# The outputs of a chunked delta rule made in transposed form by the matmuls themselves

## The chip, the cores and the metric

The kernel runs on one core of one Trainium2 chip. The metric is device microseconds for one execution, and the smaller it is the better. The engines that matter here are TensorE (PE, matmuls; its weight loads are listed as PEld), VectorE (DVE), ScalarE (ACT), GpSimd (POOL) and SyncE (SP), which issues DMAs. Each engine runs its own list of instructions in order; semaphores tie the lists together. Matmuls write PSUM, a small memory of banks that PE adds into; everything else lives in SBUF, which has 128 partitions.

## The reference, cut to what matters

There are 4 batches, 8 heads, 768 tokens and 48 numbers to a head. Each (batch, head) carries a 48 x 48 state through its tokens; the outputs of the heads, side by side (8 x 48 = 384), are the rows of a feed-forward layer.

```python
for t in range(S):
    y[:, :, t] = einsum('bhd,bhde->bhe', q[:, :, t], state)
    v_old = einsum('bhde,bhd->bhe', state, k_n[:, :, t])     # k_n: k of length 1
    state = state + beta_t * einsum('bhd,bhe->bhde', k_n[:, :, t], v_t - v_old)
x = y.transpose(0, 2, 1, 3).reshape(3072, 384)
out = gelu_exact(x @ w_in) @ w_out      # w_in 384 x 2048, w_out 2048 x 384, float64 in memory
```

## The kernel before

**Tiling.** The tokens are cut into 12 chunks (c = 0 to 11) of C = 64. A chunk has two units (a = 0, 1); a unit is two batches, whose 2 x 64 tokens fill the 128 partitions. Inside a chunk the recurrence is solved in closed form, as small matmuls, one for each batch and head. Heads go in four pairs j, r being the head within the pair and p the batch within the unit; D = 48, H = 8, NP = 4 pairs, NM = 3 blocks of 128 model columns, NF = 16 blocks of 128 hidden columns.

**The state steps of a chunk**, in order (`state_steps`, L792):

- `against_state` (L651): the product psK (L667) of both units: Kt (keys, transposed: the head's numbers in partitions, tokens in columns) and Qt (queries, likewise) are weights of 48 rows and 64 columns, the state St of 48 columns moves through them. Each unit has its own PSUM tile, for the key half and the query half.
- `subtract` (L672): DVE makes W from psK and V; ACT copies the query half out of PSUM as `y` (L679), 128 x 384 in one copy a unit. L684 is the second step of W on DVE.
- `solve` (L691): psU = Zf . W (L702), and ACT's copies of it, `U` (L710, L712). Zf is the inverse of a triangular matrix of the chunk, made ahead for two chunks at a time.
- `outputs` (L760): `use` (L717) makes psY = P . U (L732), with P (tokens by tokens, masked) as weights of 64 columns and U of 48 columns moving; `update` makes the step of the state (L743); `next_state` adds it to St on DVE; `read` (L750) makes x = psY + y on DVE, three additions a unit (L758). For chunks 0 and 1 `read` is three copies on ACT.
- `turns` (L782): six transposes of 128 x 128 on PE (L788), x being tokens by model columns, into the PSUM tile psX, and one ACT copy, 128 x 768, to xT (model columns by tokens), for which the layer waits. Chunks 0, 1 and 2 use `turn` (L766) instead, one call a unit; in chunk 1, y is added there by PE.

**Made ahead.** `load_blocks` brings keys and queries as 32 x 32 blocks; `turned_k` (L397, L399) and `turned_q` (L402) transpose them on DVE to Kt and Qt. Kt has six slots, that is three chunks. `grams` (L419) makes psG = Kt . Kt, `queries` (L437) psP = Kt . Qt, which DVE multiplies by the mask to P (L450). The helper `products` (L414) does the matmuls of both, 64 columns and 64 moving, so the profile shows both under the name psG. psG's copies to SBUF are queued with `put_off` and given out by `copy_out` (L570) at times of the plan. The rows of the triangular inverse are pairs of DVE instructions (L501, L503), its joining is psJ (L593), with 32-row operands.

**The layer.** For chunks 2 to 11 the two matrix products of the layer (fc1: xT by w_in, fc2: the result by w_out) are made in a form with seven products in place of eight, on halves. `mix_x` (L879) makes the sums of xT on DVE (L884); the parts are called P1, P5, P6, P2, R11, P7, R22, P3, R12, P4 and R21 (`part_of_layer`, L906), in four blocks of four hidden columns (psX, psZ, psY, psV, L916), then the second layer (L859). P7 writes psY, DVE adds pu into G from it (L947), and P4 writes the same PSUM again. `behind` chains all these products to one line on PE, so none can overtake another. Chunks 0 and 1 have the plain form (fc1 L811 psH, fc2 L829 psO).

**Order.** The layer of chunk w - 1 is made while the state steps of chunk w run; such a stage is some 46 to 51 us. A written plan (L1196 to L1304) gives each step a due time in units of stages (`at`, L1054; `state_at`, L1189, for the state steps), and `emit` (L1062) writes the instructions in the order of these times. DVE runs in exactly that order (`manual_schedule`, last lines). `together` (L623) chains the PE instructions of several steps, `keep` (L899) holds an ACT instruction at its place; the order of PE, ACT and SP is otherwise the scheduler's. The plan's lines that matter: even stages have `join_steps` j0, j1, j2 for the pair of chunks (w, w + 1) and the grams of w + 2 and w + 3; odd stages have none. `query(w)` is the queries' product of chunk w.

**PSUM.** The pool `dn` (L72) has two slots of two banks each; psK, psU, psY with psS, psG, psP, psJ and psX of `turns` take turns in them. `mlp`, `z` and `sq` belong to the layer.

**w_in.** It comes as 64-bit numbers by 24 DMAs on SP (`fetch`, L202 and L213), three for each of 8 parts of 256 hidden columns, one for each block of 128 model rows, and is decoded on DVE, ACT and POOL in the first stages.

Of the kernel before, what the change touches and what calls it, by code (L numbers as in the profile page):

```python
# [8 lines left out]
F32 = mybir.dt.float32  # L9
U32 = mybir.dt.uint32  # L10
# [9 lines left out]
def kernel(  # L20
# [35 lines left out]
    NA = B // 2  # L56
    NG = NC // 2
    NU = 2 * NA * H
    NM = DM // 128
    NF = DF // 128  # L60
    HALF = [slice(0, C), slice(C, 2 * C)]
# [10 lines left out]
    def dn(name):  # L72
        return ps.tile([128, 2, 512], F32, tag="dn", name=name)
# [109 lines left out]
    St = cpool.tile([128, NA, 2, NP, D], F32)  # L183
    nc.vector.memset(St, 0.0)
    nc.scalar.activation(lim[:, 1:2], lim[:, 0:1], ACT.Gelu)

    beta_m = cpool.tile([128, NC, NA, H], F32)


    win = moe_w_in.bitcast(U32).rearrange("(m q) (g f w) -> q g m f w", q=128, f=WC, w=2)  # L190
    wout = moe_w_out.bitcast(U32).rearrange("(f q) (n w) -> q f n w", q=128, w=2)
    w_parts = [(w_in_sb[:, g], win[:, g]) for g in range(DF // WC)]
# [9 lines left out]
    def fetch(n):  # L202
        if n >= len(w_parts):
            return
        dst, src = w_parts[n]
        if n < n_in:
            raw = stage[:, n % NS * 2 * WG:(n % NS + 1) * 2 * WG]
        else:
            raw = slots[(n - n_in) % len(slots)]
        w_raw[n] = raw.rearrange("q (n w) -> q n w", w=2)  # L210
        raw = raw.rearrange("q (m n w) -> q m n w", m=dst.shape[1], w=2)
        for m in range(dst.shape[1]):
            nc.sync.dma_start(out=raw[:, m], in_=src[:, m])  # L213
# [81 lines left out]
    def heads(ap):  # L295
        return ap.rearrange("q (j r) d -> q r j d", r=2)
# [348 lines left out]
    def pairs(ap, s):  # L645

        return ap.rearrange("q (k s r) d -> q k s r d", s=2, r=2)[:, :, s]
# [3 lines left out]
    def against_state(us):  # L651

        for u in us:
            u.W = wk.tile([128, H, D], F32, tag="W", name="W")
            u.y = None
            if u.c == 0:
                nc.gpsimd.tensor_tensor(u.W, u.V,
                                        ng[:, u.a].unsqueeze(2).to_broadcast([128, H, D]),
                                        op=ALU.mult)
                continue  # L660
            u.psK = dn("psK")[:, :, 0:2 * NP * D].rearrange("q r (x j d) -> q x r j d", x=2, d=D)
            for x in range(2):
                for j in range(NP):
                    for r, p in QUADS:
                        rows = slice(r * C, r * C + D)
                        to = HALF[p ^ (j % 2)] if x and u.c > 1 else HALF[p]
                        nc.tensor.matmul(u.psK[to, x, r, j, :], lhsT=(u.Qt if x else u.Kt)[rows, p, j, :],  # L667
                                         rhs=St[rows, u.a, p ^ r, j, :], start=True, stop=True)
        if us[0].c > 2:
            subtract(us)  # L670

    def subtract(us):  # L672

        for u in us:
            if u.c == 0:
                continue
            u.y = wk.tile([128, H, D], F32, tag="y", name="y")
            nc.vector.tensor_tensor(heads(u.W), u.psK[:, 0], heads(u.V), op=ALU.subtract)
            nc.scalar.copy(heads(u.y), u.psK[:, 1])  # L679
        for u in us:  # L680
            if u.c == 0:
                continue
            gm = gms[u.c // 2][:, u.t]
            nc.vector.tensor_tensor(u.W, u.W, gm.unsqueeze(2).to_broadcast([128, H, D]),  # L684
                                    op=ALU.mult)
# [4 lines left out]

    def solve(us, copies=(nc.scalar.copy, nc.scalar.copy)):  # L691
        psU = dn("psU")
        for u in us:
            zf = Zf[(u.c // 2) % 2]
            if u.c == 0 and u.a:
                psU = dn("psU")
            u.psU = quarters(psU[:, :, u.a * NP * D:(u.a + 1) * NP * D])
            for k in range(NP // 2):
                for r in range(2):
                    for p, s in SIDES:  # L700
                        h = 4 * k + 2 * s + r
                        nc.tensor.matmul(u.psU[HALF[p ^ s], s, k, r, :],  # L702
                                         lhsT=zf[HALF[p], u.t * H + h, :],
                                         rhs=u.W[HALF[p], h, :], start=True, stop=True)
        for u, copy in zip(us, copies):
            solved(u, copy)
# [41 lines left out]
            nc.vector.tensor_tensor(St[:, u.a], St[:, u.a], u.psS, op=ALU.add)  # L748

    def read(u, copy=nc.scalar.copy):  # L750
        u.x = wk.tile([128, H, D], F32, tag="x", name="x")
        both = slice(0, 128)
        for to, at_, s in ((both, both, 0), (HALF[0], HALF[1], 1), (HALF[1], HALF[0], 1)):
            dst, src = pairs(u.x[to], s), u.psY[s][at_]
            if u.c < 2:
                copy(dst, src)
            else:
                nc.vector.tensor_tensor(dst, src, pairs(u.y[at_], s), op=ALU.add)  # L758

    def outputs(us):  # L760
        use(us)
# [4 lines left out]
    def turn(u):  # L766
        if u.a == 0:
            xTs[u.c] = wk.tile([128, NM, NA * 128], F32, tag="xT", name="xT")
        xT = xTs[u.c]
        psX = sq("psX", NM, 128)  # L770
        for m in range(NM):
            cols = slice(m * 128, (m + 1) * 128)
            if u.c == 1:

                for i, part in enumerate((u.x, u.y)):
                    nc.tensor.matmul(psX[:, m, :], lhsT=part.rearrange("q h d -> q (h d)")[:, cols],
                                     rhs=ident, start=i == 0, stop=i == 1)
            else:
                nc.tensor.transpose(psX[:, m, :], u.x.rearrange("q h d -> q (h d)")[:, cols], ident)
        nc.scalar.copy(xT[:, :, u.a * 128:(u.a + 1) * 128], psX)  # L780

    def turns(us):  # L782
        c = us[0].c
        xT = xTs[c] = wk.tile([128, NM, NA * 128], F32, tag="xT", name="xT")
        psX = dn("psX")[:, :, 0:DM].rearrange("q a (m n) -> q a m n", n=128)
        for u in us:
            for m in range(NM):
                nc.tensor.transpose(psX[:, u.a, m, :],  # L788
                                    u.x.rearrange("q h d -> q (h d)")[:, m * 128:(m + 1) * 128], ident)
        keep(nc.scalar.copy, xT.rearrange("q m (a n) -> q a m n", n=128), psX)  # L790

    def state_steps(c, first=(), second=()):  # L792
        us = [tiles[c, a] for a in range(NA)]
        return [(together, (against_state, us), *first), (together, (solve, us), *second),
                (outputs, us), (together, (turns, us))]


    FH = NF // 2
# [390 lines left out]
    def state_at(c, *times, first=(), second=()):  # L1189

        steps = state_steps(c, first, second)
        if len(times) > len(steps):
            steps = steps[:-1] + [(turn, tiles[c, a]) for a in range(NA)]
        return [(t, step) for t, step in zip(times, steps) if t is not None]

    plan = [at(c + 1 + 0.25 * (c == 1), c + 2 + 0.25 * (c == 0), ffn_steps(c)) for c in range(NC)]  # L1196
# [30 lines left out]
    for c in range(4, NC):  # L1227
# [37 lines left out]
    for w in range(3, NC):  # L1265
        two_ahead = w + 2 < NC
        if w % 2:
# [10 lines left out]
            elif two_ahead:  # L1278
# [56 lines left out]
```

## Time and profile before

| what | value |
|---|---|
| median of 3 runs | 639.91 us (639.57 to 640.15) |
| the profiled execution: first to last instruction (span) | 638.7 us |
| mean granted clock of PE, as a share of full speed | 0.985 |
| instructions in the trace | 22156 |
| busy share of PE, DVE, ACT, POOL | 97%, 78%, 41%, 10% |
| L902 on ACT, copy of psX to xT, 9 of them | 0.80 us each; ACT idle 124.3 us before them in sum |
| data moved by DMA | 39.79 MB, 62 GB/s on the mean |

The profiled execution has no time of its own beside its span, which lies 1.2 us under the median. Times of single instructions below count from the span's start. In the lines of a profile, `out<-in` are the names of the tiles, `128*128` the weights' rows by columns, `128x192` the moving tile, and `x16` the number of instructions in the group; each float32 matmul of the code is two instructions. A matmul's busy time overlaps that of the next, so what one costs is read from start to start. On the page the tenths are the busy share of 40 slices, 16 us each. `[0.28 <-PE psK L667]` behind a line is the time that the engine had waited, and for what.

### The profile page before, as it was taken

To read this page: it belongs to the slowest core of one execution; us is meant where nothing else is said; L and a number is where in the kernel's file an instruction comes from. 1 tells how busy PE (TensorE), PEld (TensorE's weight loads), DVE (VectorE), ACT (ScalarE), POOL (GpSimd) and SP (SyncE) were. 2 spreads that over 40 slices of the span, in tenths; PEclk is the share of its full clock that TensorE was granted. 3 is DMA by queue.
4 is the path that set the end of the run, shared out by engine and by line. 5 is a ranking of instruction groups with operands and counts; after the bars stand their busy time and mean duration, and the time that the engine had idled before them with its cause. 6 is when DMAs were issued, how large, how long until landed. Compare 5 with 4: busy or idle time off the path is not lost.

```text
span 638.7 us, 22156 instructions
## 1 busy us (share of the span) xinstructions
PE 618.4 (97%) x9702; PEld 573.8 (90%) x9702; DVE 496.6 (78%) x1011; ACT 259.9 (41%) x586; POOL 64.9 (10%) x58
## 2 busy tenths in 40 slices
PE   6779999999999999999999999999999999999997
PEld 5667776776899999999999999999999999999997
DVE  6999989999799987999677999577999565354342
ACT  3576877624541265132265132265142253231230
POOL 4044002100300012001012001012001000000000
PEclk9977999999999999999999999999999999999999
DMA  9794884303442234221335222311222300100101
GB/s 134 172 280 139 149 175 137 50 1 73 73 67 44 47 51 77 56 36 36 58 48 79 54 27 47 57 27 28 52 29 38 62 4 2 26 2 3 26 2 25
DMA packets 158433, 39.79 MB, mean 62 GB/s; under 512 B 150016, under 2 KB 153216, under 8 KB 158336
## 3 DMA queue, kind: packets, MB, share of 16 engines
q1 hardware_dynamic: 155664, 37.34, 30.2%
q8 instruction: 76, 1.25, 0.8%
q10 hardware_dynamic: 2672, 1.03, 0.8%
q14 instruction: 21, 0.17, 0.1%
HBM read 33.62 MB, written 4.72 MB: 60 GB/s over the span
## 4 chain that ended last, share of the span: by engine, by line
PE 81%; DVE 11%; ACT 2%; DMA 2%; issue 2%; POOL 0%; SPq 0%; DVEq 0%; ACTq 0%; POOLq 0%
PE psX L859 12%; PE psY L916 11%; PE psX L916 8%; PE psY L859 8%; PE psV L916 5%; PE psZ L916 5%; PE psG L414 5%; PE psZ L859 4%; PE psV L859 4%; PE psK L667 3%; PE psO L829 3%; PE psJ L593 2%; DVE tmp L501 2%; DVE Nu L503 2%; PE psH L811 2%; PE psY L732 2%
## 5 line engine op out<-in xcount | busy, mean ns | idle before, releaser
L916 PE MATMUL psX<-xT,w_in_sb 128*128 128x128 f32 x480 | 64.5, 277 | 0.0
L503 DVE TENSOR_TENSOR Nu<-Nu,tmp 128x58 f32<-128x58 f32 (+13 forms) x168 | 58.5, 348 | 5.8
L501 DVE TENSOR_TENSOR tmp<-Nu 128x58 f32<-128x58 f32 (+13 forms) x168 | 59.2, 352 | 4.4
L916 PEld LDWEIGHTS psX<-xT,w_in_sb 128*128 128x128 f32 x480 | 58.8, 192 | 1.2 <-issue 0.3
L902 ACT COPY xT<-psX 128x768 f32<-128x768 f32 x9 | 7.2, 799 | 124.3 <-PE psX L788 124.3
L351 POOL TENSOR_TENSOR n<-n,half 128x16 f32<-128x16 f32 x10 | 30.2, 3020 | 247.2 <-DVE n L349 197.4
L859 PE MATMUL psX<-w_out_sb,G 128*128 128x192 f32 x320 | 55.3, 326 | 0.0
L859 PEld LDWEIGHTS psX<-w_out_sb,G 128*128 128x128 f32 x320 | 52.1, 190 | 0.0
L811 PE MATMUL psH<-xT,w_in_sb 128*128 128x256 f32 x192 | 44.4, 384 | 1.5 <-ACT G L902 1.3
L829 PE MATMUL psO<-w_out_sb,G 128*128 128x384 f32 x128 | 43.9, 490 | 0.0
L811 PEld LDWEIGHTS psH<-xT,w_in_sb 128*128 128x128 f32 x192 | 35.7, 190 | 8.8 <-ACT G L902 2.2
L916 PE MATMUL psY<-xT,w_in_sb 128*128 128x128 f32 x320 | 42.3, 275 | 0.0
L902 ACT COPY pu<-psZ 128x512 f32<-128x512 f32 x40 | 23.5, 587 | 39.5 <-PE psZ L916 39.5
L916 PEld LDWEIGHTS psY<-xT,w_in_sb 128*128 128x128 f32 x320 | 38.9, 192 | 0.0
L829 PEld LDWEIGHTS psO<-w_out_sb,G 128*128 128x128 f32 x128 | 23.6, 190 | 14.0
L902 ACT ACTIVATE G<-G 128x512 f32<-128x512 f32 x40 | 25.2, 629 | 20.5 <-DVE G L947 19.8
L376 POOL TENSOR_TENSOR V<-V,n 128x384 f32<-128x384 f32 x18 | 17.2, 965 | 135.3 <-DMA V<-in_v_dram 131.1
L939 DVE TENSOR_TENSOR psY<-psY,pu 128x512 f32<-128x512 f32 x20 | 14.0, 699 | 20.5 <-PE psY L916 18.7
L859 PE MATMUL psZ<-T,pu 128*128 128x192 f32 x160 | 28.6, 332 | 0.0
L859 PE MATMUL psY<-T,G 128*128 128x192 f32 x160 | 28.6, 332 | 0.0
L859 PE MATMUL psV<-w_out_sb,G 128*128 128x192 f32 x160 | 27.7, 326 | 0.0
L859 PE MATMUL psX<-T,G 128*128 128x192 f32 x160 | 27.6, 326 | 0.0
(183 smaller groups left out, 1349.7 us busy)
## 6 DMA issues: line engine op xcount, KB each, us to landing
Kp<-in_k_dram SPq DMA_DIRECT2D x76, 96.0 KB, 3.1
w_out_sb<-in_moe_w_in_dram SPq DMA_DIRECT2D x24, 256.0 KB, 4.1
w_raw<-in_moe_w_out_dram SPq DMA_DIRECT2D x16, 384.0 KB, 4.8
V<-in_v_dram SPq DMA_DIRECT2D x48, 96.0 KB, 3.1
out_dram<-o_sb SPq DMA_DIRECT2D x40, 96.0 KB, 2.2
Qp<-in_q_dram SPq DMA_DIRECT2D x64, 32.0 KB, 2.1
Qp<-in_q_dram SPq DMA_DIRECT2D x16, 96.0 KB, 4.4
Qp<-in_k_dram SPq DMA_DIRECT2D x32, 32.0 KB, 2.2
```

The lines of the kernel that those rows point to most:

```text
L351: nc.gpsimd.tensor_tensor(flat, flat, half, op=ALU.pow)
L376: engine.tensor_tensor(u.V, u.V, ns[u.c][:, u.a].unsqueeze(2).to_broadcast([128, H, D]), op=ALU.mult)
L414: nc.tensor.matmul(psG[HALF[p], r, i * NP + j, :], lhsT=u.Kt[rows, p, j, :], rhs=(u.Qt if x else u.Kt)[rows, p, j, :], start=True, stop=True)
L501: nc.vector.tensor_tensor(tmp, nu[:, j + 1:, j:j + 1].to_broadcast([128, n, j]), nu[:, j:j + 1, 0:j].to_broadcast([128, n, j]), op=ALU.mult)
L503: nc.vector.tensor_tensor(nu[:, j + 1:, 0:j], nu[:, j + 1:, 0:j], tmp, op=ALU.add)
L667: nc.tensor.matmul(u.psK[to, x, r, j, :], lhsT=(u.Qt if x else u.Kt)[rows, p, j, :], rhs=St[rows, u.a, p ^ r, j, :], start=True, stop=True)
L811: nc.tensor.matmul(psH, lhsT=w_in_sb[:, f // 2, m, f % 2 * 128:(f % 2 + 1) * 128], rhs=xTs[c][:, m, :], start=(m == 0), stop=(m == NM - 1))
L829: nc.tensor.matmul(u.psO, lhsT=G[:, u.a, f, :], rhs=w_out_sb[:, f, :], start=(f == 0), stop=(f == NF - 1))
L859: nc.tensor.matmul(ps_, lhsT=lhs[:, f, :], rhs=rhs[:, f, :], start=first and f == 0, stop=f == FH - 1, skip_group_check=not first)
L902: i = fn(*args, **kw)
L916: nc.tensor.matmul(ps_[:, i], lhsT=lhs[:, f // 2, f % 2 * 128:(f % 2 + 1) * 128], rhs=rhs, start=first and i == 0, stop=True, skip_group_c ...
L939: nc.vector.tensor_tensor(L1["Y1"], L1["Y1"], L1["pu"][:, 0], op=ALU.add)
```

## The change

Three things change.

1. **The order of model columns.** x, its transpose xT and the rows of w_in change from "head after head" to: block m (0 to 2), half r (0, 1), and in each half 48 places for head 2m + r and 16 places (PAD) for a third of head 6 + r. So heads 0 to 5 lie where the small matmuls can write them directly, at partitions 0 and 64, and heads 6 and 7 are spread over the free 16 rows of the three blocks. w_in's rows are loaded in that order, with four DMAs a part instead of three.
2. **Chunks 2 to 11 make Y transposed.** `against_state` makes only the key half of psK, one PSUM tile for both units. `of_state`, in `solve` ahead of psU, makes St . Qt into psY, with St as weights (48 columns) and Qt moving (64). `of_chunk` adds U . P into the same psY, with U as weights (48 columns) and P moving (64), then the step of the state into psS. `turned_outputs` takes the place of `outputs` and `turns`: four ACT copies take heads 6 and 7 to a tile `last`; six DMAs of 16 rows by 1 KB move these into xT's free rows (three issued by ACT, three by SP); four ACT copies take heads 0 to 5 straight to xT. The additions L758, the transposes L788, psX's copy and the copies of `y` are gone there. Chunks 0 and 1 keep the old way in the new order of columns, with five ACT copies a unit in `read` instead of three, and two for `y` in chunk 1 instead of one.
3. **The plan.** Due times of a few steps move.

```diff
@@ w_in
-    win = moe_w_in.bitcast(U32).rearrange("(m q) (g f w) -> q g m f w", q=128, f=WC, w=2)
+    HW = (H - 2) * D
+    win = [(slice(r * C, r * C + D), moe_w_in[0:HW].bitcast(U32).rearrange(
+        "(m r q) (g n) -> r q g m n", r=2, q=D, n=2 * WC)[r]) for r in range(2)]
+    win += [(slice(r * C + D, (r + 1) * C), moe_w_in[HW:].bitcast(U32).rearrange(
+        "(r m q) (g n) -> r q g m n", r=2, q=PAD, n=2 * WC)[r]) for r in range(2)]
...
+            for to, of in src:
+                nc.sync.dma_start(out=raw[to], in_=of)
@@ against_state
-            u.psK = dn("psK")[:, :, 0:2 * NP * D].rearrange("q r (x j d) -> q x r j d", x=2, d=D)
-            for x in range(2):
+            if u.c == 1 or u.a == 0:
+                psK = dn("psK")
...
+            u.psK = parts if u.c == 1 else parts[u.a:u.a + 1]
+            for x, ps_ in enumerate(u.psK):
@@ solve
         psU = dn("psU")
+        if us[0].c > 1:
+            of_state(us)
@@ read (now chunks 0 and 1 only)
+        u.x = wk.tile([128, NM, 2, C], F32, tag="x", name="x")
+        copy(u.x[:, 0::2, :, 0:D], u.psY[0])
+        for to, at_ in ((HALF[0], HALF[1]), (HALF[1], HALF[0])):
+            copy(u.x[to, 1, :, 0:D], u.psY[1][at_, 0])
+            copy(u.x[to, :, :, D:].rearrange("q m r e -> q r m e"),
+                 u.psY[1][at_, 1].rearrange("q r (m e) -> q r m e", m=NM))
@@ new
+    def of_state(us):
+        psY = us[0].psY = dn("psY").rearrange("q p (a j t) -> q p a j t", a=NA, t=C)
+        for u in us:
+            for j in range(NP):
+                for r, p in QUADS:
+                    rows = slice(r * C, r * C + D)
+                    to = slice((r ^ p) * C, (r ^ p) * C + D)
+                    nc.tensor.matmul(psY[to, p, u.a, j, :], lhsT=St[rows, u.a, p ^ r, j, :],
+                                     rhs=u.Qt[rows, p, j, :], start=u.a == j == 0, stop=True,
+                                     skip_group_check=u.a + j > 0)
+    def of_chunk(us):
...
+                    nc.tensor.matmul(psY[to, p, u.a, j, :], lhsT=u.U[HALF[p], 2 * j + r, :],
+                                     rhs=u.P[HALF[p], 2 * j + r, :], start=False, stop=True,
+                                     skip_group_check=True)
+            update(u)
+    def turned_outputs(us):
+        c, psY = us[0].c, us[0].psY
+        together((of_chunk, us))
+        for u in us:
+            next_state(u)
+        last = wk.tile([128, NA * 128], F32, tag="x", name="last")
+        xT = xTs[c] = wk.tile([128, NM, NA * 128], F32, tag="xT", name="xT")
...
+        for p, to, at_ in sides:
+            keep(nc.scalar.copy, last_p[to, p], psY[at_, p, :, NM])
+        for m in range(NM):
+            for r, queue in enumerate((nc.scalar, nc.sync)):
+                at_ = r * C + m * PAD
+                queue.dma_start(out=xT[r * C + D:(r + 1) * C, m, :], in_=last[at_:at_ + PAD, :])
+        for p, to, at_ in sides:
+            keep(nc.scalar.copy, of_p[to, p], psY[at_, p].rearrange("q a j t -> q j a t")[:, 0:NM])
@@ state_steps
-        return [(together, (against_state, us), *first), (together, (solve, us), *second),
-                (outputs, us), (together, (turns, us))]
+        steps = [(together, (against_state, us), *first), (together, (solve, us), *second)]
+        if c < 2:
+            return steps + [(outputs, us)] + [(turn, u) for u in us]
+        return steps + [(turned_outputs, us)]
@@ plan
-             state_at(2, None, 2.772, 2.851, 2.906, 2.922),
+             state_at(2, None, 2.772, 2.851),
...
-        t = {4: 2.7262, 5: 2.955}.get(c, c - (1.77 if c % 2 == 0 else 2.57))
+        t = {4: 2.7262, 5: 2.955}.get(c, c - (1.77 if c % 2 == 0 else 2.6))
         plan += [at(t, t + 0.0005, [(1.0, turned_k, u) for u in us])]
...
-            plan += [state_at(w, w + 0.367, w + 0.59, w + 0.72, w + 0.93, second=query(w))]
+            plan += [state_at(w, w + 0.367, w + 0.59, w + 0.72, first=query(w))]
...
-                     state_at(w, w + 0.465, w + 0.58, w + 0.72, w + 0.93, second=[j2] + gram(w + 3))]
+                     state_at(w, w + 0.465, w + 0.58, w + 0.72, first=gram(w + 3), second=[j2])]
...
-                plan += spread("gram", 4, w + 0.63)
+                plan += spread("gram", 4, w + 0.48)
```

More of the change, by code (lines that the diff above doesn't have):

```diff
@@ L58 @@
     NU = 2 * NA * H
+    PAD = C - D
     NM = DM // 128
@@ L182 @@
     G = cpool.tile([128, NA, NF, 128], F32)
-    St = cpool.tile([128, NA, 2, NP, D], F32)
+    St = cpool.tile([128, NA, 2, NP, D], F32, name="St")
     nc.vector.memset(St, 0.0)
@@ L187 @@
     beta_m = cpool.tile([128, NC, NA, H], F32)
-    win = moe_w_in.bitcast(U32).rearrange("(m q) (g f w) -> q g m f w", q=128, f=WC, w=2)
+    HW = (H - 2) * D
[3 more added lines that the diff above has]
+        "(r m q) (g n) -> r q g m n", r=2, q=PAD, n=2 * WC)[r]) for r in range(2)]
     wout = moe_w_out.bitcast(U32).rearrange("(f q) (n w) -> q f n w", q=128, w=2)
-    w_parts = [(w_in_sb[:, g], win[:, g]) for g in range(DF // WC)]
+    w_parts = [(w_in_sb[:, g], [(to, of[:, g]) for to, of in win]) for g in range(DF // WC)]
     n_in = len(w_parts)
@@ L210, in fetch @@
         w_raw[n] = raw.rearrange("q (n w) -> q n w", w=2)
+        if n < n_in:
+            raw = raw.rearrange("q (m n) -> q m n", m=NM)
+            for to, of in src:
+                nc.sync.dma_start(out=raw[to], in_=of)
+            return
         raw = raw.rearrange("q (m n w) -> q m n w", m=dst.shape[1], w=2)
@@ L660, in against_state @@
                 continue
-            u.psK = dn("psK")[:, :, 0:2 * NP * D].rearrange("q r (x j d) -> q x r j d", x=2, d=D)
-            for x in range(2):
+            if u.c == 1 or u.a == 0:
+                psK = dn("psK")
+            n = NP * D
+            parts = [psK[:, :, i * n:(i + 1) * n].rearrange("q r (j d) -> q r j d", d=D) for i in range(2)]
+            u.psK = parts if u.c == 1 else parts[u.a:u.a + 1]
+            for x, ps_ in enumerate(u.psK):
                 for j in range(NP):
@@ L665, in against_state @@
                         rows = slice(r * C, r * C + D)
-                        to = HALF[p ^ (j % 2)] if x and u.c > 1 else HALF[p]
-                        nc.tensor.matmul(u.psK[to, x, r, j, :], lhsT=(u.Qt if x else u.Kt)[rows, p, j, :],
+                        nc.tensor.matmul(ps_[HALF[p], r, j, :], lhsT=(u.Qt if x else u.Kt)[rows, p, j, :],
                                          rhs=St[rows, u.a, p ^ r, j, :], start=True, stop=True)
@@ L676, in subtract @@
                 continue
-            u.y = wk.tile([128, H, D], F32, tag="y", name="y")
-            nc.vector.tensor_tensor(heads(u.W), u.psK[:, 0], heads(u.V), op=ALU.subtract)
-            nc.scalar.copy(heads(u.y), u.psK[:, 1])
+            nc.vector.tensor_tensor(heads(u.W), u.psK[0], heads(u.V), op=ALU.subtract)
+            if u.c == 1:
+                u.y = su.tile([128, NM, 2, C], F32, tag="y", name="y")
+                nc.scalar.copy(u.y[:, :, :, 0:D].rearrange("q m r d -> q r m d"), u.psK[1][:, :, 0:NM])
+                nc.scalar.copy(u.y[:, :, :, D:].rearrange("q m r e -> q r m e"),
+                               u.psK[1][:, :, NM, :].rearrange("q r (m e) -> q r m e", m=NM))
         for u in us:
@@ L750, in read @@
     def read(u, copy=nc.scalar.copy):
[L751 to L758, printed above, removed]
+        u.x = wk.tile([128, NM, 2, C], F32, tag="x", name="x")
@@ new lines, in of_chunk @@
+    def of_chunk(us):
+        psY = us[0].psY
+        psS = dn("psS")[:, :, 0:NA * NP * D].rearrange("q i (a j d) -> q i a j d", a=NA, d=D)
+        for u in us:
+            u.psS = psS[:, :, u.a]
+            for j in range(NP):
+                for r, p in QUADS:
+                    to = slice((r ^ p) * C, (r ^ p) * C + D)
+                    nc.tensor.matmul(psY[to, p, u.a, j, :], lhsT=u.U[HALF[p], 2 * j + r, :],
+                                     rhs=u.P[HALF[p], 2 * j + r, :], start=False, stop=True,
+                                     skip_group_check=True)
+            update(u)
@@ new lines, in turned_outputs @@
+    def turned_outputs(us):
+        c, psY = us[0].c, us[0].psY
+        together((of_chunk, us))
+        for u in us:
+            next_state(u)
+        last = wk.tile([128, NA * 128], F32, tag="x", name="last")
+        xT = xTs[c] = wk.tile([128, NM, NA * 128], F32, tag="xT", name="xT")
+        of_p = xT.rearrange("q m (a p t) -> q p m a t", a=NA, t=C)
+        last_p = last.rearrange("q (a p t) -> q p a t", a=NA, t=C)
+        sides = [(p, *(slice(x * C, x * C + D) for x in (r, r ^ p))) for p in range(2) for r in range(2)]
+        for p, to, at_ in sides:
[6 more added lines that the diff above has]
+            keep(nc.scalar.copy, of_p[to, p], psY[at_, p].rearrange("q a j t -> q j a t")[:, 0:NM])
@@ L771, in turn @@
         for m in range(NM):
[L772 to L779, printed above, removed]
-        nc.scalar.copy(xT[:, :, u.a * 128:(u.a + 1) * 128], psX)
[L782 to L790, printed above, removed]
+            parts = (u.x, u.y) if u.c == 1 else (u.x,)
+            for i, part in enumerate(parts):
+                part = part[:, m].rearrange("q r d -> q (r d)")
+                if u.c == 1:
+                    nc.tensor.matmul(psX[:, m, :], lhsT=part, rhs=ident, start=i == 0, stop=i == 1)
+                else:
+                    nc.tensor.transpose(psX[:, m, :], part, ident)
+        nc.scalar.copy(xT[:, :, u.a * 128:(u.a + 1) * 128], psX)
     def state_steps(c, first=(), second=()):
         us = [tiles[c, a] for a in range(NA)]
-        return [(together, (against_state, us), *first), (together, (solve, us), *second),
-                (outputs, us), (together, (turns, us))]
+        steps = [(together, (against_state, us), *first), (together, (solve, us), *second)]
+        if c < 2:
+            return steps + [(outputs, us)] + [(turn, u) for u in us]
+        return steps + [(turned_outputs, us)]
     FH = NF // 2
@@ L1191, in state_at @@
         steps = state_steps(c, first, second)
-        if len(times) > len(steps):
-            steps = steps[:-1] + [(turn, tiles[c, a]) for a in range(NA)]
         return [(t, step) for t, step in zip(times, steps) if t is not None]
```

## The prediction, made before the changed kernel ran

> **What bounds the kernel now.** I read the page's busy times and 40 slices first, then the timeline of single engines in three stages, then the waits. The page (busy us; below them tenths per slice of 16 us):
>
> ```profile
> PE 618.4 (97%) x9702; PEld 573.8 (90%) x9702; DVE 496.6 (78%) x1011; ACT 259.9 (41%) x586; POOL 64.9 (10%) x58
> ...
> PE   6779999999999999999999999999999999999997
> ...
> DVE  6999989999799987999677999577999565354342
> ACT  3576877624541265132265132265142253231230
> ```
>
> TensorE (PE) is full from the fifth slice to the last but one. Busy time by windows has it at 51.00 of 51.00 us from 318 to 369 and from 407 to 458, and the list of PE's waits names nothing later than 139 us (0.47 us, for DVE's XM). So behind 139 us a PE instruction that goes shortens the end by its pitch, and any new PE wait lengthens it whole. Before 139 us VectorE (DVE) has hardly a gap from 47 us on, and PE waits for it. The span is 638.7 us and the median of the three runs 639.91, so I work out a difference and subtract it from 639.91.
>
> **What goes from PE.** The timeline of PE in one stage (start, length, line, operation, count):
>
> ```profile
> 436.38 1.15 PE L702 MATMUL psU<-W,Zf 64*64 64x48 f32 x64
> 437.46 1.15 PE L593 MATMUL psJ<-Zf,XM 32*64 32x64 f32 x32
> 438.54 1.16 PE L414 MATMUL psG<-Kt 48*64 48x64 f32 x64
> 439.63 2.87 PE L859 MATMUL psZ<-T,pu 128*128 128x192 f32 x16
> ...
> 454.94 0.82 PE L788 MATMUL psX<-ident,x 128*128 128x128 f32 x6
> 455.60 2.77 PE L859 MATMUL psV<-w_out_sb,G 128*128 128x192 f32 x16
> ```
>
> From start to next start six transposes cost 0.66 us; chunk 2's cost 0.33 twice. Ten chunks: **-6.6 us**.
>
> The small matmuls keep their number: 32 instructions of Q with the state and 32 of P with U for each unit, before and after (each matmul of the code is two), now with 48 columns of weights and 64 moving instead of 64 and 48. The trace has no such shape. It has 64 and 48 (psU above, 436.38 to 437.46: 1.08 us for 64) and 64 and 64 (psG, 438.54 to 439.63: 1.09). Without the step to another row height behind it (0.15) that is 0.93 for 16 groups of four, 58 ns a group. Moving columns below the weights' number cost nothing, then. Above it they do: with 128 columns of weights 128 moving go at 0.89 us for 8 and 192 at 2.60 for 16. So the larger side sets the pace, and here that is 64 as before. The ends: if weights alone counted, a group would take 48/64 of 58 ns, and 320 groups (32 a chunk) 4.5 us less; dearer than 64 and 64 fewer weights can hardly be, so +0.2 (the 0.01 in 20 batches). I take **0**, the row of 64 and 64.
>
> [...]
>
> In even stages 4, 6 and 8 the grams of chunk w+3 go from behind psJ (32 rows) to behind psK (64 rows). One change of row height, about 0.15 us, goes from each: **-0.4**. Together the gain is 7.0 us.
>
> **What new waits come.** DVE runs in the order of the plan (the code schedules it by hand), and two of its steps now stand ahead of L947, whose end lets the next product (P4, psY<-TX,w_in_sb) write Y1.
>
> Odd stages: the queries' mask product L450 moves with `first=query(w)` from w+0.59 to w+0.367, ahead of L947 (P7 of block 1, which falls at w+0.41). DVE's timeline in stage 9, and PE's:
>
> ```profile
> 475.81 1.02 DVE L684 TENSOR_TENSOR W<-W,gm 128x384 f32<-128x384 f32 x2
> 476.75 0.38 DVE L501 TENSOR_TENSOR tmp<-Nu 128x220 f32<-128x220 f32 x1
> 477.16 0.39 DVE L503 TENSOR_TENSOR Nu<-Nu,tmp 128x220 f32<-128x220 f32 x1
> 477.47 0.68 DVE L947 TENSOR_TENSOR G<-psY,pu 128x512 f32<-128x512 f32 x1
> ...
> 486.02 1.22 DVE L450 TENSOR_TENSOR P<-psG,mask 128x1024 f32<-128x1024 f32 x1
> 487.16 0.32 DVE L501 TENSOR_TENSOR tmp<-Nu 128x168 f32<-128x168 f32 x1
> ```
> ```profile
> 478.27 1.10 PE L916 MATMUL psY<-TX,w_in_sb 128*128 128x128 f32 x8
> ```
>
> L947 ends at 478.15, P4 starts at 478.27: 0.12 us to spare. L450 takes 1.14 of DVE. P4 then starts 1.0 late. Stages 5 and 7 stand alike (L947 ends at 285.55, P4 at 285.67; 381.85 and 381.97). In stage 3 the margin is 0.8, so 0.3; in stage 11 DVE waits for P7 itself, so nothing. **+3.3.**
>
> Even stages: `turned_k` of chunk w+3 moves from w+0.43 to w+0.40, ahead of L947, and its grams now follow psK at once on PE. But it writes Kt slots that psK(w) still reads (six slots, three chunks live). DVE's timeline in stage 8, psK having started at 429.79:
>
> ```profile
> 428.11 0.69 DVE L947 TENSOR_TENSOR G<-psY,pu 128x512 f32<-128x512 f32 x1 [0.28 <-PE psY L916]
> ...
> 430.53 0.71 DVE L399 STREAM_TRANSPOSE Kt<-Kb 128x512 f32<-128x512 f32 x1 [0.28 <-PE psK L667]
> 431.47 0.71 DVE L399 STREAM_TRANSPOSE Kt<-Kb 128x512 f32<-128x512 f32 x1 [0.22 <-PE psK L667]
> ```
>
> So L399 can't be early: unit 0 ends 1.45 behind psK's start, unit 1 at 2.1. psK, halved, is through at 0.97; grams of unit 0 wait 0.5, of unit 1 another 0.2, and P4 0.1 for L947, which now ends at 2.8. Some 0.8 in stages 4, 6, 8: **+2.4**. On DVE the W steps queue behind it (2 us later), but psU now starts 0.9 later behind the state product, and W is there by then.
>
> **What is hidden.** DVE loses six additions (2 x 1.09 = 2.2 us) per chunk late in the stage, where PE waits for none: 0. ACT loses two y copies and xT's (0.48 x 2 + 0.80 = 1.8) and gets eight copies, by the rows 128x192 at 0.32 and 128x384 at 0.48 about 0.26 x 4 + 0.48 x 4 = 3.0, and three DMA issues at 0.55 (its own out issues). It stood idle for 12.2 us ahead of xT's copy in stage 8 and 15.0 in stage 9; without that cover P1 would wait for the 2.9 more. The six DMAs of 16 KB land in about 2.1 (the page's 32 KB rows of Qp, the nearest); psY ends at 447.0, xT is needed at 457.3. Even in series with the copies (1.3 + 1.6 + 3) they fit. The DMAs wait for ACT's first copies, so SP and ACT wait at their issues: behind SP's three stand later loads and the stores to `out`, of which none is needed within this stage (the next Kp loads are due a stage later); behind ACT's three stand only its four larger copies, counted here.
>
> [...]
>
> PSUM: psY lives from the state product to ACT's last copy, in one of two dn slots. In chunk 2 its slot is psP's, freed by L450, which ends at 152.92, while the solve starts at 151.23: 1.7 at most, 0 if fc2's 14 psO products go ahead. Chunks 0 and 1 read with 20 ACT copies for 12 (0.3 us more per unit) and SP issues 32 w_in loads for 24 (0.43 each); DVE's chain before 139 us has 0.7 to 1.5 us of room at those places. I take **+0.7** for both, with 0 and 3 as ends.
>
> Sum: -7.0 + 3.3 + 2.4 + 0.7 = -0.6: **639.3 us**.
>
> **Rivals.**
> - *The waits don't come* (L450 or L399 costs PE nothing, because P4, the grams or psK are placed elsewhere: PE's and ACT's order isn't written by hand). Then -7.0 + 0.7: 633.6. For it: PE can be given what is ready. Against: nothing else is ready there, since the products form one line and P4 is its next. 0.26.
> - *Slower: SP holds xT back.* SP issues in order. In chunk 2 it issues 16 Qp loads from 155.81 to 164.8. If xT's three stand behind them, the first goes at 164.8 and lands 0.45 + 2.1 later, at 167.4, against P1 at 165.1 less the 0.7 saved by then: +3.0, so 642.3. It decides from an issue later than 161.9. Against: outputs do stand between such loads at 502.3. Had odd stages it too (8 loads to 502.2, P1 at 503.4), 2 more each. 0.17.
> - *The new shape runs by its weights*: 639.3 - 4.5 = 634.8. For it the equal cost of 48 and 64 moving, against it the 192 row. 0.05.
>
> **Numbers.** My case has 0.52 and by its own terms 637.5 to 641. A measurement of this kernel tells some 0.2% (1.3 us) from no change. A quarter of my case lies below 638.6, little above 641.2. Faster 0.26 + 0.05 + 0.13 = 0.44; same 0.36; slower 0.17 + 0.03 = 0.20. The range of 633.0 to 643.0 takes in the three rivals' times; past it lie the outer part of the first and SP's odd stages, under 0.2.
>
> **What would show it.** PE without L788, psK x64 in all; the Q product with the state x64 in about 0.95 us beside psU; in stages 5, 7, 9 P4 waiting about 1 us for DVE's L947, in 4, 6, 8 psG waiting for Kt inside the psK batch; no wait of P1 for xT. I am wrong if PE stays at 51.00 of 51.00, if 64 small ones take other than 0.9 to 1.1 us, or if the first psX product of a stage waits for a DMA.

## The result, and the profile after

| | median us | runs | lowest to highest |
|---|---|---|---|
| before | 640.12 | 16 | 639.39 to 641.17 |
| changed | 641.83 | 16 | 639.40 to 646.70 |

The ratio is 1.0031, 95% interval 1.0017 to 1.0044: the changed kernel is slower by 2.0 us (1.1 to 2.8). The forecast was 639.3, slightly faster, and slower had 0.20. The runs of the changed kernel also lie further apart (7.3 us from lowest to highest, before 1.8). The profiled execution is one of the longest: span 642.6, 644.31 with what lies around it, 2.5 above the median.

The page of the changed kernel, busy time of the engines and tenths per slice:

```profile
PE 613.3 (95%) x9642; PEld 567.1 (88%) x9642; DVE 474.4 (74%) x951; ACT 273.5 (43%) x645; POOL 63.0 (10%) x58
...
PE   5769999999999999999999999999999999999997
...
DVE  7999899999599886998575998575998564362342
ACT  3576776624543256232266232266232253233230
...
PEclk9576999998999999999999999999999999999999
```

PE's busy time is 5.1 us less, with the 60 transpose instructions gone, and the span is longer. So PE now waits. The list of PE's waits behind 140 us (before, it was empty there):

```profile
PE psY L969 <- DVE G L1000: 2.8, 4, 0.9
PE psG L424 <- DVE Kt L409: 1.4, 3, 0.5
PE psU L720 <- DVE P L460: 1.3, 1, 1.3
PE psJ L603 <- DVE XM L522: 0.5, 1, 0.5
```

The columns are the sum in us, the number of waits and the longest. The first is P4 behind the addition that was L947 and is L1000 now; the second is the grams behind `turned_k`; the third is the solve of chunk 2. The fourth is not new: the kernel before has it too, just ahead of 140 us.

Where the time lies is seen best from marks on PE: the start of the first product P1 of each chunk's layer, and the time from one to the next. "Waits out" is a run told below (e7), in which the first two kinds of wait are removed.

| stretch | before | changed | waits out | forecast for changed less before | measured |
|---|---|---|---|---|---|
| start to P1 of chunk 2 | 165.09 | 169.82 | 166.56 | 0.0 (+0.7 - 0.66) | +4.7 |
| stage 3 | 48.85 | 48.55 | 48.11 | -0.36 | -0.30 |
| stage 4 | 51.66 | 51.60 | 51.16 | 0.0 | -0.06 |
| stages 5, 7, 9, each | 45.19 | 45.54 | 44.41 | +0.34 | +0.35 |
| stages 6, 8, each | 51.11 | 51.00 | 50.54 | 0.0 | -0.11 |
| stage 10 | 48.93 | 48.16 | 48.16 | -0.66 | -0.77 |
| stage 11 | 44.21 | 43.47 | 43.47 | -0.66 | -0.74 |
| P1 of chunk 11 to the end | 42.12 | 42.38 | 42.37 | 0.0 | +0.26 |

(The description of the kernel above has a layer's first part in four blocks of four hidden columns; it is two blocks of four in each half. The forecast went by two.)

From stage 3 to stage 11 the forecast holds to some 0.1 us a stage. What it missed lies ahead of P1 of chunk 2. The 4.7 there is that of a long execution: a second profile of the changed kernel (e10, 641.38 us) has P1 of chunk 2 at 166.88, 1.8 behind the kernel before, and every later stretch the same to 0.04. Two things stand ahead of P1 of chunk 2. First, w_in. The list of DMA issues in the first 110 us, before and after (count, size of one, median us to landing):

```profile
w_out_sb<-in_moe_w_in_dram SPq DMA_DIRECT2D x24, 256.0 KB, 4.1
```
```profile
w_out_sb<-in_moe_w_in_dram SPq DMA_DIRECT2D x16, 288.0 KB, 6.6
...
w_out_sb<-in_moe_w_in_dram SPq DMA_DIRECT2D x16, 96.0 KB, 7.0
```

VectorE, which decodes w_in, now waits for it (waits of VectorE before 180 us, changed kernel):

```profile
DVE St L766 <- PE psS L761: 4.5, 1, 4.5
DVE w_e L241 <- DMA w_out_sb<-in_moe_w_in_dram: 2.5, 1, 2.5
```

The wait of 2.5 ends at 76.3 us; from there VectorE's line to the state product of chunk 2 is late, and that product starts at 142.33 for 139.76 (140.93 in e10's profile, where this wait is 1.0). Second, the solve of chunk 2 on PE, as a timeline:

```profile
152.23 1.11 PE L784 MATMUL psY<-Qt,St 48*48 48x64 f32 x64
154.63 1.96 PE L720 MATMUL psU<-W,Zf 64*64 64x48 f32 x64 [1.29 <-DVE P L460]
156.52 6.15 PE L882 MATMUL psO<-w_out_sb,G 128*128 128x384 f32 x16
```

psU takes the PSUM slot of psP, which the mask product L460 frees; PE waits 1.29 us. And psU then takes 1.96 us for 64 where it takes 1.10 in stages 8 and 9. The windows around it say why (us, PE busy, granted clock, DMA):

```profile
152.00:153.30 1.30, 1.30 (x75) 1.00 0.58 135
153.30:154.60 1.30, 0.04 (x4) 1.00 0.26 47
154.60:158.00 3.40, 3.37 (x67) 0.50 0.76 141
158.00:162.00 4.00, 4.00 (x14) 1.00 0.54 80
```

Behind the wait the granted clock is 0.50 for 3.4 us.

### The profile page after: what moved, and what is told of

It reads as the page before. It is cut to its first block, busy times and chain, and to the rows that moved or that the text cites. A ratio compares the mean times of both kernels' runs of the same rounds, so it can differ in the third digit from the quotient of the medians.

```text
span 642.6 us, 22163 instructions
## 1 busy us (share of the span) xinstructions
PE 613.3 (95%) x9642; PEld 567.1 (88%) x9642; DVE 474.4 (74%) x951; ACT 273.5 (43%) x645; POOL 63.0 (10%) x58
## 4 chain that ended last, share of the span: by engine, by line
PE 57%; DVE 28%; DMA 7%; issue 4%; SPq 2%; ACT 1%; POOL 0%; DVEq 0%; ACTq 0%; POOLq 0%
PE psX L912 11%; PE psY L969 8%; PE psY L912 6%; DVE tmp L511 5%; PE psX L969 5%; DVE Nu L513 5%; DMA w_out_sb<-in_moe_w_in_dram 5%; PE psZ L912 4%; PE psV L969 3%; PE psZ L969 3%; PE psV L912 2%; PE psO L882 2%; PE psJ L603 2%; PE psG L424 2%; PE psU L720 2%
## 5 line engine op out<-in xcount | busy, mean ns | idle before, releaser
L955 ACT COPY last<-psY 48x128 f32<-48x128 f32 x40 | 10.4, 260 | 48.0 <-PE psY L797 47.5
L912 PE MATMUL psY<-w_out_sb,G 128*128 128x192 f32 x160 | 27.6, 326 | 0.0
```

Source lines behind the costliest of these rows:

```text
L912: nc.tensor.matmul(ps_, lhsT=lhs[:, f, :], rhs=rhs[:, f, :], start=first and f == 0, stop=f == FH - 1, skip_group_check=not first)
L955: i = fn(*args, **kw)
```

## The experiments

Three theories stood at the start. A: w_in's new loads land late. B: PE's wait in front of psU in chunk 2, and the half clock behind it, cost some 3 us. C: the waits that the forecast counted (P4 behind the mask product, the grams behind Kt) cost what the trace lists. The rival to A and B was that chunks 0 and 1 pay for the eight more ScalarE copies of `read`. Twelve runs follow. For each of those with several executions, the median stands beside the kernel before in the same runs, and the ratio with its interval.

**e1: the new loads alone, in the kernel before**

```diff
+        if n < n_in:
+            raw = raw.rearrange("q (m n) -> q m n", m=NM)
+            for to, of in src:
+                nc.sync.dma_start(out=raw[to], in_=of)
+            return
```

(Not shown: `src` is made as in the changed kernel, for 48, 48, 16 and 16 partitions.)

> The kernel before, but w_in is loaded as in the changed kernel (four DMAs a part into 48, 48, 16 and 16 partitions instead of three into 128); its rows therefore stand in the new order while x keeps the old one, so the products of the layer mix wrong rows; the work is the same. Theory A: the new loads land later (6.6 to 7.0 us after issue for 3.7 to 4.1), VectorE's decoding waits for them, and that reaches PE at the state product of chunk 2, late by up to the 2.6 us of the profiled run: 640.1 + 0.5 to 2.6. Rival: the loads are hidden, the lag comes from chunks 0 and 1 having more ScalarE copies: 640.1 within 0.3.

Measured 641.84 against 640.13, ratio 1.0029 (1.0018 to 1.0041), so +1.9 (1.2 to 2.6). VectorE waits 2.2 us for w_in, the loads land after 6.2 and 7.1 us, and the state product of chunk 2 starts at 140.95. From there to P1 the stretch is 25.33, the same as before. A holds: the loads alone cost this.

**e2: the old loads in the changed kernel**

```diff
-        if n < n_in:
-            raw = raw.rearrange("q (m n) -> q m n", m=NM)
-            for to, of in src:
-                nc.sync.dma_start(out=raw[to], in_=of)
-            return
```

(Not shown: `src` is made as in the kernel before, and the loop over three blocks that follows takes w_in's parts too.)

> The changed kernel, but w_in is loaded as before, three DMAs a part into 128 partitions each; the rows stand in the old order, x in the new, so the products mix wrong rows; the work is the same. Theory A: no wait of VectorE for w_in, the state product of chunk 2 earlier by 0.5 to 2.6: 641.8 less that, 639.2 to 641.3, with less spread between runs. Rival (copies of chunks 0 and 1): 641.8.

Measured 640.55 against 640.13, ratio 1.0004 (0.9993 to 1.0015): 1.3 less than the changed kernel. The state product of chunk 2 starts at 139.41, no later than before, although chunks 0 and 1 still make their additional copies: the rival falls. The wait for w_in is gone. The wait in front of psU is there, but not the half clock. The windows of this run, around a wait as long as that above:

```profile
150.40:151.70 1.30, 0.01 (x2) 1.00 0.41 76
151.70:155.10 3.40, 3.40 (x71) 1.00 0.66 121
```

So the spell at half clock is no sure consequence of the wait.

**e3: the queries of chunk 2 earlier**

```diff
-             ... at(2.725, 2.726, [(1.0, queries, third)]),
+             ... at(2.7115, 2.7116, [(1.0, queries, third)]),
```

> The changed kernel with the queries of chunk 2 due at 2.7115 instead of 2.725, so VectorE's mask product stands ahead of two sums of w_in. Theory B: PE's wait of 1.3 us in front of psU (the PSUM slot of psP, freed by the mask product) goes, and with it the 3.3 us at half clock behind the wait (1.6 to 1.7 lost): 641.8 - 2.9 = 638.9. Rival: the half clock comes on its own time and not from the wait, so only 1.3 goes: 640.5. Second rival: the sums that now come later hold back the layer's first parts: 641.8 or more.

Measured 640.91 against 640.13, ratio 1.0007 (0.9995 to 1.0018): 0.9 less than the changed kernel, where B said 2.9 and the rival 1.3. The wait is gone from the list. From the state product of chunk 2 to P1 it is 24.50 in the profile; in the changed kernel it was 27.49 with the half clock, and 25.95 in e10's profile without it. So the wait costs 1.45 and the spell 1.55, and the spell comes in some executions only. B was right on the wait and too high on the mean price.

**e4: the mask product of odd stages behind the addition that P4 waits for**

```diff
+        elif c > 2 and c % 2:
+            left[c] = dst, psP          # the product of mask and psP is made by late_mask
...
-            plan += [state_at(w, w + 0.367, w + 0.59, w + 0.72, first=query(w))]
+            plan += [state_at(w, w + 0.367, w + 0.59, w + 0.72, first=query(w)),
+                     at(w + 0.43, w + 0.431, [(1.0, late_mask, [tiles[w, a] for a in range(NA)])])]
```

> The changed kernel with the queries' product of odd stages where it is, beside psK, but its mask product on VectorE as a step of its own at w + 0.43, behind the addition that P4 waits for. Theory C: the four waits of P4 (0.18 + 3 x 0.89 = 2.85 us) go: 641.8 - 2.85 = 639.0. Rival: the wait moves to psU, whose PSUM slot the mask product frees: 641.8.

Measured 637.57 against 640.13, ratio 0.9962 (0.9947 to 0.9977): 4.3 less than the changed kernel. Stages 5, 7 and 9 take 44.40 for 45.54, stage 3 48.10 for 48.55, 3.9 in sum. VectorE and PE in stage 9, first the changed kernel, then this one:

```profile
481.59 1.22 DVE L460 TENSOR_TENSOR P<-psG,mask 128x1024 f32<-128x1024 f32 x1
...
483.44 0.68 DVE L1000 TENSOR_TENSOR G<-psY,pu 128x512 f32<-128x512 f32 x1
```
```profile
484.18 1.16 PE L969 MATMUL psY<-TX,w_in_sb 128*128 128x128 f32 x8 [0.89 <-DVE G L1000]
```
```profile
478.30 0.68 DVE L1010 TENSOR_TENSOR G<-psY,pu 128x512 f32<-128x512 f32 x1
...
480.36 1.22 DVE L467 TENSOR_TENSOR P<-psG,mask 128x1024 f32<-128x1024 f32 x1
```
```profile
479.12 1.08 PE L979 MATMUL psY<-TX,w_in_sb 128*128 128x128 f32 x8
```

With the addition ahead of the mask product P4 doesn't wait. The listed wait was 0.89, the stage pays 1.14, since the products around an idle PE lose their overlap, which the list of waits doesn't count: the product ahead of the wait runs out its 1.06 where the next would start after 0.89, and P4's successor starts 1.00 behind it and not 0.92. C holds, and the wait did not move to psU.

**e5 and e6: why the loads are slow.** Both are the kernel before with other loads of w_in, one execution each.

```diff
 # e5: four DMAs, all into 128 partitions
+            if n < n_in and m == 2:
+                for f in (slice(0, WC // 2), slice(WC // 2, WC)):
+                    nc.sync.dma_start(out=raw[:, m, f], in_=src[:, m, f])
+                continue
 # e6: two DMAs, 64 partitions each
+        if n < n_in:
+            for p in range(2):
+                nc.sync.dma_start(out=raw[HALF[p]]..., in_=src[HALF[p]]...)
```

> The kernel before, with w_in's parts loaded by four DMAs into all 128 partitions (the third of the three cut in two by columns). Theory A1 (the narrow destination makes the loads slow): they land 3.7 to 4.2 us after issue as before, and VectorE doesn't wait for w_in. Theory A2 (the number of DMAs, 32 for 24, does): they land at 6 us or more and VectorE waits some 2 us.

> The kernel before, with w_in's parts loaded by two DMAs into 64 partitions each (384 KB a DMA, 16 DMAs in all). A1: they land later than their size explains, 6 us or more, and VectorE waits for w_in by some 2 us. A2: fewer DMAs, no wait of VectorE for w_in.

Times 640.75 and 640.83 against 640.08, both within what the kernel before scatters. The issue lists, e5 first:

```profile
w_out_sb<-in_moe_w_in_dram SPq DMA_DIRECT2D x16, 256.0 KB, 4.0
w_out_sb<-in_moe_w_in_dram SPq DMA_DIRECT2D x16, 128.0 KB, 4.1
```
```profile
w_out_sb<-in_moe_w_in_dram SPq DMA_DIRECT2D x16, 384.0 KB, 7.2
```

32 DMAs into the full width land as before; 16 into the half width land as late as the changed kernel's. So A2 is out, the number of DMAs doesn't make them slow; the narrow destination (A1) fits. One rival is left: each slow load also brings three blocks of 2 KB to a partition, and each fast one a single block, and no run has the one without the other. The traces' single packets say the same as the landings: w_in's packets of 2 KB took 84 ns in the median in the kernel before and 191 in the changed kernel. In e6 VectorE has no wait for w_in all the same, against A1's expectation: its last load goes out at 64.7 and lands at 73.8, where the changed kernel's goes out at 67.8 and lands at 76.2. So here a late landing cost time only where an engine stood close behind it.

**e7: the grams of even stages behind P4**, on top of e4

```diff
-        t = {4: 2.7262, 5: 2.955}.get(c, c - (1.77 if c % 2 == 0 else 2.6))
+        t = {4: 2.7262, 5: 2.955}.get(c, c - (1.77 if c % 2 == 0 else 2.585))
...
-                     state_at(w, w + 0.465, w + 0.58, w + 0.72, first=gram(w + 3), second=[j2])]
+                     state_at(w, w + 0.465, w + 0.58, w + 0.72, second=[j2])]
+            plan += [at(w + 0.4905, w + 0.491, [(1.0, together, *gram(w + 3))])] if two_ahead else []
...
-                plan += spread("gram", 4, w + 0.48)
+                plan += spread("gram", 4, w + 0.4945)
```

> The changed kernel with the later mask product of the run before (637.6 us), and in even stages turned_k at w + 0.415 (behind the addition that P4 waits for) and the grams of chunk w + 3 as a step of their own at w + 0.49, behind P4 instead of inside the batch of psK; their copies at w + 0.4945. Theory C: the three waits of psG for Kt (0.46 each, by stage some 0.6) go: 637.6 - 1.4 to 2.0 = 635.6 to 636.2. Rival: psU's PSUM slot is psG's, and psU now waits for psG's four copies on ScalarE: 637.6 or more.

Measured 635.84 against 640.08, ratio 0.9934 (0.9921 to 0.9946): 1.7 less than e4. Stages 4, 6 and 8 are shorter by 0.46 each than the changed kernel's, and the wait is gone: C holds again, and psU doesn't wait for the copies. The 0.46 is not the price of the wait, though: the grams now stand between two products of 128 rows, so that two more changes of row height come in (below). This is the column "waits out" above.

**e8: both, the queries of e3, and w_in's loads ahead of other loads**

```diff
+    def after_w_in(fn, *args):     # its DMAs are placed behind the last of w_in's
...
-    at(1.06, 1.065, [(1.0, load, 3)])
+    at(1.31, 1.315, [(1.0, after_w_in, load, 3)])
-    at(1.07, 1.071, [(1.0, load_v, 2)])
+    at(1.3, 1.301, [(1.0, after_w_in, load_v, 2)])
```

> The run before (mask product and grams later), with the queries of chunk 2 early and with the loads of chunk 3 and of V, and the key blocks of chunk 4, issued behind the last of w_in's, so that their small packets don't stand among w_in's. If all terms add up: 636.0 less 1.3 for the slot in front of psU, less up to 1.5 for w_in: 633.2 to 634.7. Rival: w_in's last part lands late by itself, and its wait of some 2.5 us on VectorE stays: 634.7 to 635.

Measured 634.84 against 640.08, ratio 0.9918 (0.9904 to 0.9931). It is the fastest whole kernel of the study, 5.2 us (4.4 to 6.1) ahead of the kernel before. The loads still land at 5.9 and 7.2 us.

**e12: the same without the new order of the loads**

> The changed kernel with the mask product and the grams later and the queries of chunk 2 early, and nothing done on the loads. Against the run that has w_in's old loads besides (632.6 us), it gives the price of the new loads where PE has no other added wait: by the pairs measured so far 1.3 to 1.7, so 633.9 to 634.3. If the order of the other loads was worth something, it lies above the 634.8 of the run that has it.

Measured 635.26 against 640.18, ratio 0.9924 (0.9911 to 0.9936). The order of the other loads brings 0.4, within what the runs scatter. In the profiles of e3, e4 and e8 VectorE waits only 0.5 to 0.6 us for w_in and in e12's not at all, and yet the state product of chunk 2 starts at 139.5 to 140.9, against 138.7 to 139.9 in the kernels whose loads are 128 wide. ScalarE waits 1.0 us for Kp in the changed kernel and 1.2 in e12, and not in the kernel before. Of the other loads of the first 110 us w_out's land after 5.5 us in the median in the changed kernel, for 4.8 before, V's and Qp's after 4.0, for 4.5 and 4.4. By which wait the price reaches PE in these kernels isn't shown.

**e9: every added wait and the new loads undone**

> The changed kernel with every added wait taken out (mask product and grams later, queries of chunk 2 early) and with w_in loaded as before by three DMAs into 128 partitions (rows in the old order, so the layer's products mix wrong rows; the work is the same). It shows what making Y transposed brings by itself. The forecast's terms say 640.1 - 7.0 = 633.1; by the stages of the profiles, 0.77 us for each of ten chunks, 632.4. If something else of the change still costs (the copies of chunks 0 and 1, the free rows' DMAs), it stays above 633.5.

Measured 632.62 against 640.39, ratio 0.9880 (0.9866 to 0.9895): -7.7 (6.7 to 8.6). That is what making Y transposed is worth by itself; its profile has 6.9 of it behind the start of chunk 2's state product, and the rest ahead of it, where the kernels with old loads scatter by 1.2. Against e12, which has the new loads, it is 2.6 less; the pairs before to e1 and changed to e2 gave 1.7 to 1.9 and 1.3.

**e10: the changed kernel again**

> The changed kernel once more, unaltered, beside the run before this on one chip: 641.8. By theory its profile shows the wait of 1.29 us in front of psU again, behind it about 3.4 us at half clock or none (two of four profiles with this wait had it), and the state product of chunk 2 at 140.5 to 142.5 us.

Measured 642.34 against 640.39, ratio 1.0031 (1.0020 to 1.0043), the result again. Its profile has the wait of 1.3 in front of psU at full clock, and the state product of chunk 2 at 140.93.

**e11: both halves of the partitions at once**

```diff
-            for to, of in src:
-                nc.sync.dma_start(out=raw[to], in_=of)
+            for i, (to, of) in enumerate(src):
+                (nc.scalar if i % 2 else nc.sync).dma_start(out=raw[to], in_=of)
```

> The fastest whole kernel so far (634.8 us: mask product and grams later, queries of chunk 2 early, other loads behind w_in's), with the loads of the lower half's rows (partitions 0 to 63) issued by SP and those of the upper half's by ScalarE, so that both halves are in flight together. If a load is slow because at any time only one half of the partitions is written, landings come down from 5.9 and 7.2 us to 4 to 5, and the time falls to 632.6 to 633.5. Rival: each narrow load is slow by itself, landings stay at 6 or more: 634.8, or more for the 16 issues of some 0.45 us on ScalarE.

Measured 650.63 against 640.18, ratio 1.0163 (1.0139 to 1.0186). Landings stay at 6.1 to 6.7, so the rival's reading is the better one: a narrow load is slow by itself, also beside one into the other half. And the time rises by 16 over e8; ScalarE's waits behind its issues sum to 17. ScalarE's timeline:

```profile
38.79 5.91 ACTq L231 DMA_DIRECT2D w_out_sb<-in_moe_w_in_dram  x4
44.74 1.08 ACT L417 COPY Kt<-psT 128x512 f32<-128x512 f32 x2 [5.37 <-DMA w_out_sb<-in_moe_w_in_dram]
```

Four issues hold it for 5.91 us, and the copy that PE needs stands behind them. The profile puts 5.37 us of that copy's idle time down to the landing of a w_in load.

## Why the forecast was wrong

Point by point, with the steps as the prediction put them.

**Right: what bounds the kernel.** Behind P1 of chunk 2 each instruction taken from PE shortened a stage and each wait lengthened it.

**Right: the gain.** Forecast -7.0 for the transposes and row heights. Stages 10 and 11, where no wait came, give 0.77 and 0.74 a chunk for the 0.66 forecast, the odd stages without waits 0.78. The even stages of "waits out" give only 0.57, since e7 puts the grams between two products of 128 rows; in the changed kernel itself the even stages are 0.11 shorter with a wait that costs 0.80 (below), so 0.91 without it: 0.77 and 0.14 for the row height. All together e9 has -7.7.

**Right: the shape of 48 columns and 64 moving.** 64 of them go in 0.93 us (488.77 to 489.70 in stage 9), so 58 ns a group, the row of 64 and 64. The rival in which the weights alone set the pace is out.

**Right in kind, nearly in size: the mask product ahead of L947.** Forecast +3.3; 3.9 by the stages, 4.3 by the medians. The 1.0 of late start is 0.89 of listed wait and 0.25 of lost overlap.

**Right: the grams behind Kt.** Forecast +2.4 at 0.8 a stage. PE in stage 8, and the same pair without a wait in stage 9:

```profile
434.74 1.15 PE L680 MATMUL psK<-St,Kt 48*64 48x48 f32 x64
436.35 1.20 PE L424 MATMUL psG<-Kt 48*64 48x64 f32 x64 [0.46 <-DVE Kt L409]
437.57 1.16 PE L969 MATMUL psY<-TX,w_in_sb 128*128 128x128 f32 x8
```
```profile
477.43 1.15 PE L680 MATMUL psK<-St,Kt 48*64 48x48 f32 x64
478.40 1.13 PE L424 MATMUL psG<-Qt,Kt 48*64 48x64 f32 x64
479.46 1.16 PE L969 MATMUL psX<-xT,w_in_sb 128*128 128x128 f32 x8
```

From psK to the product of 128 rows it is 2.83 with the wait and 2.03 without: 0.80 a stage for the 0.46 that the list has. VectorE's two transposes end 1.46 and 2.06 behind psK's start, for 1.45 and 2.1 forecast. e7 wins back only 0.46 a stage of it (1.4, by the medians 1.7), because its place for the grams costs the rest.

**Right: what is hidden.** P1 waits for no xT. In chunk 2 SP issued xT's three DMAs at 165.35, in the middle of the Qp loads and not behind them, and P1 came at 169.82, so the rival in which SP holds xT back is out.

**Wrong: "I take +0.7 for both, with 0 and 3 as ends".** This is the step that turned the sign. It held two terms, and each is larger than the whole.

- *The PSUM slot in chunk 2.* The mechanism was named, with 1.7 at most, and then discounted in case fc2's products go ahead. (It gave the slot to psY; `solve` asks for psU first, so it is psU that waits.) They didn't go ahead: `together` orders psJ, psY and psU, the psO products were placed behind psU, and PE idles. The wait is 1.3, it costs 1.45 by the profiles (0.6 to 1.4 by the medians of e3 and e12 against their partners), and in two of the five profiles that have it PE then ran 3.4 us at half clock, for another 1.55.
- *w_in's loads.* They were priced as SP's issues, 32 of 0.43 us for 24, and set against 0.7 to 1.5 us of room. The landing wasn't asked for: 6.6 and 7.0 us for 4.1, with the same bytes. That costs 1.3 to 2.6 by three pairs of kernels. The copies of chunks 0 and 1, priced in the same sentence, cost nothing that shows in e2.

With -6.9 (e9's profile: stages 3 to 11 -6.2, the stretch of chunk 2 -0.9, the end +0.2), +3.9 and +1.4 (what e4 and e7 took out), +1.45, 0.6 (two fifths of 1.55) and about +1.7 the sum is +2.1, against 2.0 measured. With the slot at the 0.6 to 1.4 of the medians it is 0.7 to 1.5, so the sum is good to about one microsecond. Forecast and measured differ by 2.5 to 2.6, and this step by 0.7 against 3.8 (2.3 to 3.1 with the medians).

Two things stay open: the 0.26 us at the end, which no run looked into, and the way by which the late loads reach PE. VectorE's wait is one; but PE's granted clock is also low from 28 to 62 us, on the mean 0.67 to 0.80 in three profiles whose loads are 128 wide (before, e2, e5) and 0.64 to 0.75 in six with the new loads (the changed kernel, e1, e3, e4, e7, e8), and no run holds that still. Nor is it shown what in the chip makes a narrow load slow.

## What to carry to other kernels

A load with the same bytes is not the same load: ask for its landing time in the shape that it will have (here 4.1 us into 128 partitions, 6.6 into 48 and 7.0 into 16), and in a kernel like this one keep loads 128 partitions wide when an engine runs close behind them. A step that takes work from a full engine pays only as far as the new waits in its neighbours are cleared; here the places of two steps in a written plan held 6 us, and with them moved (e7) the same change was 0.7% faster than the kernel before instead of 0.3% slower. A wait cost more than its listed length here: 1.14 for 0.89, 0.80 for 0.46. A first stage that is paced by another engine needs its own sum, with each unknown at the size that its mechanism gives and not at a small value between the ends.

## What the runs showed of the hardware

- **Narrow loads.** In the stretch from 28 to 46 us the DMA engines of the kernel before were busy 0.88 and moved 259 GB/s; in the changed kernel they were busy 0.93 and moved 187. w_in's loads into 128 partitions landed in 4.0 to 5.1 us in the median (before, e2, e5, e9); into 64, 48 or 16, with three blocks to a partition, in 5.4 to 7.2. w_in's packets of 2 KB took 84 ns in the median before and 191 in the changed kernel. With loads into both halves of the partitions issued together (e11) they landed in 6.1 to 6.7. No run shows the cause.
- **The clock.** A PE idle for 1.3 us was followed by 3.4 us at 0.50 in two of five profiles (the changed kernel, e4; not e2, e7, e10), and idle times of 0.89 were not in the three of the changed kernel (stages 5, 7 and 9, at 1.00). In each of the traces of the kernel before and of the changed kernel the changes of the granted clock lie whole multiples of 3.413 us apart (before at 39.33, 56.40 and 636.66, changed at 14.66, 35.13, 38.55, 41.96, 45.38, 59.03, 154.60 and 158.01). How much idle time falls into one such interval doesn't settle what follows: 1.26 us of it, from 151.19 to 154.60 in the changed kernel, was followed by 0.50, while 1.66 from 79.51 to 82.92 (PE waits 1.90 us for ScalarE there) and 1.68 from 63.23 to 66.64 in the kernel before were followed by 1.00. No run moved the wait on purpose, and what brings the spell isn't shown.
- **ScalarE at a DMA issue.** Four issues took it 5.9 us (e11), and everything in its list waited: the copy behind them stood idle for 5.37 us, which the profile puts down to the landing of a w_in load.
